# Sixteen transform tiles laid out by the groups of the last inverse stage, with a new order of the steps

## The chip, the core and the metric

The kernel runs on one core of a Trainium2 chip. The metric is the device time of one execution in microseconds. Five engines work side by side, each through its own list of instructions in order: TensorE (PE, matmuls; PEld is its weight load), VectorE (DVE), ScalarE (ACT), GpSimd (POOL) and SyncE (SP), which here only issues transfers. An engine waits for another, or for a transfer, by semaphores.

## The reference

```python
x = A_x                                          # [1, 2048, 512], float32
g = sigmoid((x * gate_w).sum(-1, keepdims=True))
a = irfft2(rfft2(x) * (w_r + 1j * w_i), s=(2048, 512))
h = gelu(einsum("bsd,df->bsf", x, w1) + b1)      # D 512, F 1792, tanh form
b = einsum("bsf,fd->bsd", h, w2) + b2
return g * a + (1 - g) * b
```

## The kernel before

Branch a is a two-dimensional Fourier transform, a product with W and the inverse; branch b is an MLP; the gate g mixes them.

The 2048 rows are taken as 16 tiles of 128. Matmuls transform along the 512 columns (`pd`, `ph`, `py`) and, at the end, along the 128 rows of a tile and back along the columns (`pz`, `pa`, `po`); between them a 16-point transform runs *across* the tiles, on DVE, as two stages of radix 4 forward and two inverse. The tile `y` holds all of it: 128 partitions, 16 tiles `Y[j]`, two components each, 257 columns. The groups of four tiles are

- `stage1(j0)`: tiles j0, j0+4, j0+8, j0+12, on DVE;
- `filt(q0)`: the second forward stage, the product with W (`m`, L771), `merge` (L780) and the first inverse stage, on tiles 4·q0 to 4·q0+3, on DVE;
- `stage4(j0)`: the last inverse stage, on tiles j0, j0+4, j0+8, j0+12, on DVE (temporaries `d0…` to `d3…`, by group).

In each radix-4 step (`radix4`) the last two writes are paired: one instruction writes a component of the group's second tile and one of its fourth (`mixed`), as one access with a stride between the two (`y<-d1d,d1d` is the first paired write of group 1, into tiles 5 and 13; `y<-d1s` the second).

After a group's `stage4` its four rows 64 are corrected: SP reads them from the four tiles into the small tile `ownx` (L813), ACT scales a copy `ownz` (L814), DVE combines the two (L816), and SP writes them back (L819). `ownx3` is the one of group 3, tiles 3, 7, 11 and 15. Then `inverse(c, h)` takes the tiles: ACT makes `sw` from `y` (L832), DVE `pq` (L836), TensorE `pz`.

The MLP's matmuls use a scheme of sums and differences (tiles `uxB`, `nuB`, `fiveB`, `g_…`, `v…`). The raw rows of w2 arrive in `vr…` (L999, issued by SP); ACT copies half of one into `v0…` (L1006), and DVE forms `vs…` from both (L1004). The results of branch b go to the accumulator `bacc` in memory.

All of this is first recorded as a graph of 2146 steps. Each step belongs to one engine. A written table, `ORDER` (L122), lists the steps in the order in which they are emitted, and `SLOTS` (L208) gives each buffer its place in its pool. `schedule()` asserts that the order respects the true dependencies, which it knows by parts of buffers (three for each tile of `y`). The costs that `a`, `v`, `m` and `dma` hand to a step belong to the planner that made the table; with a table written out they move nothing. On emission a layer below adds the semaphore waits, from the memory that the instructions touch.

Of the kernel before, what the change touches and what calls it, by code (L numbers as in the profile page):

```python
# [16 lines left out]
P = 128  # L17
# [32 lines left out]
def _split(v):  # L50
    h = _round12(v)
    return h.astype(np.float32), _round12(np.asarray(v, np.float64) - h).astype(np.float32)


def _tables():
# [47 lines left out]
    for n in range(NJ):  # L103
        for r in range(2):
            for c in range(2):
                y = np.zeros((2, 2))
                y[r, c] = 0.5
                u = (y[0, 0] - y[1, 1]) + 1j * (y[1, 0] + y[0, 1])
                v = ((y[1, 0] - y[0, 1]) + 1j * (y[0, 0] + y[1, 1])) * -1j * np.exp(1j * np.pi * n / NJ)
                for q in range(4):  # L110
                    o = np.array([u, v]) * np.exp(-0.5j * np.pi * (n // 4 * q % 4))
                    fx[r, n, c, :, n % 4 + 4 * q] = np.stack([o.real, o.imag], 1)
# [238 lines left out]
def tile_kernel(ctx: ExitStack, tc: tile.TileContext, xt, xc, w1, w2, b1, b2, x0g, wf, wrev, out, consts):  # L351
# [229 lines left out]
    def forward(j):  # L581
# [67 lines left out]
        if j // 4 == 3:  # L649
            for k in range(2):  # L650
                o = j % 4 * 2 + k
                add("sp", 0.58, 5.0, lambda k=k, o=o: sp.dma_start(own.ap()[o * 8:o * 8 + 8, :ND], yy.ap()[0:P:HP, j % 4::4, k]),
                    [Y[i] for i in range(j % 4, NJ, 4)], [(own, o)])

# [724 lines left out]
```

## Time and profile before

| | |
|---|---|
| runs | 362.92, 364.76, 365.01 us, median 364.76 |
| the profiled execution | 364.13 us |
| its span, and what lies outside it | 362.3 us, 1.83 us |
| mean granted TensorE clock | 0.988 |
| instructions in the span | 5797 |
| HBM | 52.02 MB read, 17.31 MB written |

The span runs from the first to the last instruction of the trace. An engine is busy while one of its instructions runs; issuing transfers does not count. The granted clock is the share of full speed that TensorE's throttle allowed. In the rows, `ownx<-y` means that `ownx` is written from `y`, with the numbers of buffers left out.

### The profile page before, as it was taken

The numbers are of one execution on the slowest core, as the hardware profiler recorded it, in microseconds if no ns is written. First come the engines' busy times: TensorE is split into PE (matmuls) and PEld (weight loads), VectorE is DVE, ScalarE is ACT, GpSimd is POOL, SyncE is SP. The second block draws the span as 40 slices with busy tenths as digits, with TensorE's granted clock in tenths as the row PEclk, the third lists the DMA queues.
The fourth block names the chain that finished last, engine by engine and source line by source line (L and its number), as shares of the span: only waits on it lengthen the run. The fifth ranks groups of instructions, "written<-read, shape, count | busy, mean of one in ns | idle before, by whom it ended". The sixth has DMA issues, their size and how long they took to land.

```text
span 362.3 us, 5797 instructions
## 1 busy us (share of the span) xinstructions
PE 348.5 (96%) x1742; PEld 293.5 (81%) x1742; DVE 337.0 (93%) x700; ACT 302.1 (83%) x631; POOL 56.5 (16%) x75
## 2 busy tenths in 40 slices
PE   6999999999999999999999999999869999999993
PEld 5988887888878888888888888888758888788782
DVE  4999998899999999999999999999678999999992
ACT  4999999999998677797888848799399999989732
POOL 1011002100013002000231400001010000443430
PEclk9999999999999999999999999999969999999998
DMA  7998969868697979998988865426756635599987
GB/s 216 358 296 207 359 193 267 180 215 231 176 302 148 281 213 224 254 318 218 249 211 219 145 152 189 154 88 233 148 102 178 177 130 161 88 155 213 170 184 238
DMA packets 47719, 74.63 MB, mean 206 GB/s; under 512 B 5544, under 2 KB 18344, under 8 KB 47688
## 3 DMA queue, kind: packets, MB, share of 16 engines
q1 hardware_dynamic: 37528, 58.42, 49.8%
q0 software_dynamic: 9728, 15.51, 26.9%
q10 hardware_dynamic: 432, 0.33, 0.3%
q8 instruction: 14, 0.23, 0.3%
q14 instruction: 17, 0.14, 0.1%
HBM read 52.02 MB, written 17.31 MB: 191 GB/s over the span
## 4 chain that ended last, share of the span: by engine, by line
PE 90%; ACT 3%; DMA 2%; DVE 1%; issue 1%; SPq 1%; DVEq 0%; ACTq 0%
PE po L416 36%; PE uxA L416 9%; PE uxB L416 9%; PE nuB L416 7%; PE nuA L416 7%; PE pd L416 4%; PE pz L416 4%; PE ph L416 3%; PE py L416 3%; PE pa L416 3%; PE dx L416 2%; DMA cf<-cf 1%; DMA bacc<-s 1%; PE dn L416 1%; PE dm L416 1%
## 5 line engine op out<-in xcount | busy, mean ns | idle before, releaser
L964 ACT ACTIVATE po<-s 128x512 f32<-128x512 f32 x40 | 23.7, 602 | 1.8 <-DVE g_6l L472 0.8
L425 ACT ACTIVATE s<-po 128x512 f32<-128x512 f32 x40 | 23.4, 596 | 0.9 <-PE po L416 0.9
L832 ACT ACTIVATE sw<-y,keep 64x512 f32<-64x512 f32 x32 | 22.7, 720 | 0.6
L771 DVE TENSOR_TENSOR m<-y,wf 128x514 f32<-128x514 f32 x32 | 21.3, 689 | 0.4
L416 PEld LDWEIGHTS pd<-cf,w 128*128 128x128 f32 x128 | 17.8, 190 | 3.8 <-DVE cf L543 2.0
L416 PE MATMUL pd<-cf,w 128*128 128x129 f32 x128 | 19.2, 276 | 1.7 <-DVE cf L543 1.7
L416 PE MATMUL py<-zb,tf 128*128 128x258 f32 x96 | 20.3, 297 | 0.0
L416 PEld LDWEIGHTS pz<-tg,pq 128*128 128x128 f32 x128 | 18.3, 195 | 1.6
L416 PE MATMUL pz<-tg,pq 128*128 128x128 f32 x128 | 19.0, 278 | 0.0
L416 PE MATMUL pa<-zb,ci 128*128 128x256 f32 x96 | 17.9, 297 | 0.9 <-ACT od L425 0.9
L416 PEld LDWEIGHTS pa<-zb,ci 128*128 128x128 f32 x96 | 14.9, 192 | 3.8 <-ACT od L425 1.5
L416 PE MATMUL nuB<-xB,wB0h 128*128 128x512 f32 x56 | 17.5, 393 | 0.0
L416 PEld LDWEIGHTS py<-zb,tf 128*128 128x128 f32 x96 | 15.9, 189 | 2.0
L974 ACT ACTIVATE s<-po,b2t 128x512 f32<-128x512 f32 x16 | 11.2, 699 | 6.8 <-PE po L416 6.6
L416 PE MATMUL uxB<-xBt,wB 128*128 128x512 f32 x42 | 12.0, 430 | 4.5 <-DVE nuB L1227 4.5
L589 DVE TENSOR_TENSOR eo<-xf 128x256 f32<-128x256 f32 x32 | 12.7, 418 | 3.5 <-DMA xf<-in_x0g 3.4
L416 PE MATMUL nuA<-xA,wA0h 128*128 128x512 f32 x48 | 14.9, 392 | 0.0
L628 DVE TENSOR_TENSOR zb<-pd,zb 128x256 fp32r<-128x256 f32 x32 | 13.3, 419 | 0.9 <-ACT logit L627 0.9
L410 POOL DMA_DIRECT2D wA0l<-in_w x6 | 5.1, 847 | 57.6 <-ACT wA0l L477 25.3
L416 PEld LDWEIGHTS uxB<-xBt,wB 128*128 128x128 f32 x42 | 8.5, 208 | 6.6 <-DVE nuB L1227 4.9
L648 ACT ACTIVATE y<-pys 64x257 f32<-64x257 f32 x32 | 12.9, 415 | 0.5
L836 DVE TENSOR_TENSOR pq<-y,sw 128x256 f32<-128x256 f32 x32 | 12.8, 417 | 0.4 <-ACT sw L832 0.2
(595 smaller groups left out, 1274.3 us busy)
## 6 DMA issues: line engine op xcount, KB each, us to landing
wf<-in_wf SPq DMA_DIRECT2D x16, 257.0 KB, 3.8
xf<-in_xt SPq DMA_DIRECT2D x14, 256.0 KB, 5.6
tf<-tf SPq DMA_DIRECT2D x16, 192.0 KB, 4.0
wrA<-in_w SPq DMA_DIRECT2D x12, 256.0 KB, 4.7
xbA<-in_xc SPq DMA_DIRECT2D x8, 256.0 KB
xbB<-in_xc SPq DMA_DIRECT2D x8, 256.0 KB, 4.5
bacc<-s SPq DMA_DIRECT2D x8, 256.0 KB
w<-bacc POOLq DMA_DIRECT2D x8, 256.0 KB, 5.0
```

The source lines that it names most:

```text
L410: return add("pool", 0.92, 3.3, lambda: nc.gpsimd.dma_start(dst(), src(), accum_op=ALU.add), reads, writes, 2.2 * kb / 350)
L416: pe.matmul(ps, w, x, start=start, stop=stop, **more)
L425: a(lambda: act.activation(o.ap(), i.ap(), AF.Copy, scale=scale), n, [i], [o])
L589: v(lambda s=s, op=op: vec.tensor_tensor(eo.ap()[:, s], x.ap()[:, 0:2], x.ap()[:, 2:4], op=op), 256, [x], [(eo, s)])
L628: v(lambda c=c: vec.tensor_tensor(segs(xl, c), both(c), segs(xh, c), op=ALU.subtract), 256, [ps[c], (xh, c)], [(xl, c)])
L648: a(lambda o=o, i=i: act.activation(Y[j].ap()[o:o + HP, 1], pys.ap()[i:i + HP, 1], AF.Copy), 257, [(pys, 1)], [(Y[j], 1 + k)], more=0.07)
L771: v(lambda mk=mk, k=k, y=y, w=w: vec.tensor_tensor(mk.ap(), y.ap(), w.ap()[:, k:k + 1, :ND].to_broadcast([P, 2, ND]), op=ALU.mult), 514, [ ...
L832: a(lambda sw=sw, y=y, o=o, i=i: act.activation(sw.ap()[o:o + HP], y.ap()[i:i + HP], AF.Copy, scale=keep.ap()[i:i + HP]), 512, [y, keep, * ...
L836: v(lambda sw=sw, pq_=pq_, y=y, k=k, op=op: vec.tensor_tensor(pq_.ap()[:, k], y.ap()[:, k], sw.ap()[:, 1 - k], op=op), 256, [y, TURNED[c], ...
L964: a(lambda ps=ps, n=n, o=o: act.activation(ps.ap(), o.ap()[:, n], AF.Copy), size, [o], [ps], more=0.04)
L974: a(lambda o=o, ps=ps, q=q: act.activation(o.ap(), ps.ap(), AF.Identity, bias=b2t.ap()[:, q:q + 1]), 600, [b2t, ps], [o])
```

## The change

The tiles of `y` change places: tile j lies at place j % 4 · 4 + j // 4, so that the four tiles of a `stage4` group are neighbours, and those of a `filt` group lie four places apart. The accesses that name several tiles follow (the own-row reads of L652, `merge`, the read and write of rows 64, `less_y`), and so do the columns of the table `fx`, which writes all tiles' rows 0 and 64 back. The planner's figure for the `sw` copies goes from 0.165 to 0.195, and `ORDER` and `SLOTS` are made anew. The graph of steps and their dependencies are the same. Line numbers behind the new function are four higher.

```diff
+def place(j):
+    return j % 4 * 4 + j // 4
...
-                    fx[r, n, c, :, n % 4 + 4 * q] = np.stack([o.real, o.imag], 1)
+                    fx[r, n, c, :, place(n % 4 + 4 * q)] = np.stack([o.real, o.imag], 1)
...
 ORDER = """
-8 12 16 108 6 15 0 2 3 4 5 27 19 18 28 7 21 22 30 23 29 24 1 31 59 9 60 56 55 13 14 25 10 57 17 58 86 489 36 37 40 38
...
+0 2 8 15 12 108 6 9 489 1 31 32 60 18 7 19 20 28 27 30 22 21 16 17 490 59 491 13 14 10 29 23 496 62 107 55 3 56 24 58
...
-    Y = [View(yy, 3 * j, 3, lambda t, j=j: t[:, j]) for j in range(NJ)]
+    Y = [View(yy, 3 * j, 3, lambda t, j=j: t[:, place(j)]) for j in range(NJ)]
...
-    YP = [View(yy, 3 * j, 3, lambda t, j=j: packed(t[:, j])) for j in range(NJ)]
+    YP = [View(yy, 3 * j, 3, lambda t, j=j: packed(t[:, place(j)])) for j in range(NJ)]
...
-                add("sp", 0.58, 5.0, lambda k=k, o=o: sp.dma_start(own.ap()[o * 8:o * 8 + 8, :ND], yy.ap()[0:P:HP, j % 4::4, k]),
+                add("sp", 0.58, 5.0, lambda k=k, o=o: sp.dma_start(own.ap()[o * 8:o * 8 + 8, :ND], yy.ap()[0:P:HP, j % 4 * 4:j % 4 * 4 + 4, k]),
...
         def merge():
-            e = yy.ap()[:, 4 * q0:4 * q0 + 4]
+            e = yy.ap()[:, q0::4]
...
         def rows():
-            return yy.ap()[HP:HP + 1, j0::4].rearrange("p j a b -> p j (a b)")[:, :, :D]
+            return yy.ap()[HP:HP + 1, 4 * j0:4 * j0 + 4].rearrange("p j a b -> p j (a b)")[:, :, :D]
...
-                    [y, keep, *([TURNED[c]] if i else [])], [(sw, k)], more=0.165)
+                    [y, keep, *([TURNED[c]] if i else [])], [(sw, k)], more=0.195)
...
-            vec.tensor_tensor(x, x, yy.ap()[:, c + 4 * (q // 2)::8, q % 2, :2 * P], op=ALU.subtract)
+            vec.tensor_tensor(x, x, yy.ap()[:, 4 * c + q // 2:4 * c + 4:2, q % 2, :2 * P], op=ALU.subtract)
```

What the new order moves is seen in the engines' lists. First SP, about two thirds of the way through the program, where group 3's rows 64 are read. A row has the line, the kind, what is written from what, the shape, and in brackets the semaphores that the instruction waits for (DMAHW and DMASW are those of transfers). Before:

```order
L413 DMA wBtl2_3193<-su2_758 128x512 [waits DMAHW6_49,DMAHW2_49]
L813 DMA ownx3_3195<-y_322 4x1x512 [waits DMAHW7_49,DVE_49]
L999 DMA vr11_3197<-in_w2 128x512 [waits DMAHW0_49,PE_49]
L999 DMA vr12_3199<-in_w2 128x512 [waits DMAHW1_49,DMASW0_49,Activation_49]
L980 DMA bacc1_3135<-s11_774 128x512
L819 DMA y_322<-ownx3_3195 1x4x512 [waits DMAHW7_49,DMAHW3_49,DVE_49]
L825 DMA tg31_3281<-ti 128x256 [waits DMAHW4_49,PE_49]
```

The same place of the changed kernel, around its read of `ownx3`:

```order
L417 DMA wBtl2_3128<-su2_734 128x512 [waits DMAHW5_49,PE_49]
L817 DMA ownx3_3130<-y_264 4x1x512 [waits DMAHW6_49,DVE_49]
L417 DMA wBth2_3132<-su2_734 128x512 [waits DMAHW7_49,DMASW3_49,PE_49]
L417 DMA ci_3004<-ci 128x512 [waits DMAHW0_49]
L817 DMA ownx1_3203<-y_264 4x1x512 [waits DMAHW1_49,DMAHW2_49,DVE_49,Activation_49]
L823 DMA y_264<-ownx3_3130 1x4x512 [waits DMAHW6_49,DVE_49]
```

The two loads of w2 no longer stand behind the read of `ownx3`. In the changed kernel they come later on SP, behind the write back of `ownx1` (vr13 and vr12, for the same step of w2; vr11 belongs to the step before it):

```order
L823 DMA y_264<-ownx1_3203 1x4x512 [waits DMAHW7_49,DMAHW1_49,DVE_49]
L984 DMA bacc0_3279<-s02_572 128x512 [waits DMAHW0_49]
L1003 DMA vr13_3350<-in_w2 128x512 [waits PE_49]
L417 DMA wBth5_3432<-su5_1742 128x512 [waits DMAHW2_49]
L829 DMA tg11_3434<-ti 128x256 [waits DMAHW3_49,PE_49]
L417 DMA wBth6_3447<-su6_1502 128x512 [waits DMAHW4_49]
L1003 DMA vr12_3449<-in_w2 128x512 [waits DMAHW5_49,DMASW5_49]
```

Then ACT, at the step that copies vr12, `v06`. Before:

```order
L892 ACTIVATE wb4h_3191<-wb4l_raw_2918 128x512 [waits DMAHW4_49,DMAHW0_49]
L425 ACTIVATE uxB21_3202<-uxB20_3122 128x512 [waits DVE_49,PE_49]
L1006 ACTIVATE v06_3204<-vr12_3199 128x256 [waits DMAHW2_49,DMAHW1_49]
L915 ACTIVATE uxB10_2976<-uxB10_2976,b1t_350 128x512
L814 ACTIVATE ownz3_3207<-ownx3_3195,al_527 4x512 [waits DMAHW7_49,DVE_49]
L425 ACTIVATE fiveB2_3222<-nuB21_3212 128x512 [waits PE_49]
```

And in the changed kernel:

```order
L852 ACTIVATE zb0_88<-pz7_3404 128x4x128 [waits PE_49]
L836 ACTIVATE sw5_3421<-y_264,keep_1506 64x512 [waits DMAHW7_49]
L429 ACTIVATE s20_2868<-po2_200_3355 128x512 [waits PE_49]
L429 ACTIVATE s21_2805<-po2_210_3176 128x512 [waits PE_49]
L1010 ACTIVATE v06_3505<-vr12_3449 128x256 [waits DMAHW5_49,DVE_49]
L836 ACTIVATE sw13_3507<-y_264,keep_1506 64x512 [waits PE_49]
```

`v06` now stands among the steps of the last `inverse` calls, with `ownz3` far ahead of it. Third, SP at the start of the program, before (`x2` is two rows that read alike):

```order
L547 DMA b2t_80<-in_b2 128x4
L518 DMA xf4_105<-in_xt 128x256 x2
L523 DMA cf_125<-cf 128x258 x2
L491 DMA xf8_129<-in_xt 128x512
L907 DMA war0_136<-in_w1 128x256 x2
L413 DMA tf0_159<-tf 128x384
```

and changed:

```order
L551 DMA b2t_92<-in_b2 128x4
L522 DMA xf4_95<-in_xt 128x256
L911 DMA war0_97<-in_w1 128x256
L522 DMA xf4_95<-in_xt 128x256
L911 DMA war0_97<-in_w1 128x256
L527 DMA cf_124<-cf 128x258 x2
L495 DMA xf8_127<-in_xt 128x512
```

The two halves of `war0`, the first rows of w1, now go ahead of the table `cf`.

200 rows, old and new, of tables (ORDER, SLOTS) are left out of this document.

## The prediction

> **What bounds the kernel now.** I read the busy sums first, then the 40 slices, then the chain of work that ended last.
>
> ```profile
> PE 348.5 (96%) x1742; PEld 293.5 (81%) x1742; DVE 337.0 (93%) x700; ACT 302.1 (83%) x631; POOL 56.5 (16%) x75
> PEclk9999999999999999999999999999969999999998
> PE 90%; ACT 3%; DMA 2%; DVE 1%; issue 1%; SPq 1%; DVEq 0%; ACTq 0%
> ```
>
> TensorE (PE) is busy for 348.5 of 362.3 us, and 90% of the chain is PE. Only one slice inside the program, the 30th, has a granted clock below nine tenths. So TensorE sets the end, and something that makes it neither shorter nor less idle is worth nothing. The view of stretches tells where its idle time lies. Its columns are start:end, length, then busy time (count) of PE, weight loads, DVE, ACT and POOL, granted clock, DMA share and GB/s.
>
> ```profile
> 0.00:7.36 7.36, 4.55 (x12) 3.47 (x12) 2.83 (x13) 2.52 (x5) 1.71 (x12) 1.00 0.68 183
> 100.00:257.20 157.20, 157.20 (x696) 129.47 (x695) 154.92 (x299) 129.17 (x246) 24.19 (x28) 1.00 0.79 209
> 257.20:271.00 13.80, 9.33 (x40) 7.57 (x39) 8.25 (x15) 8.00 (x15) 1.72 (x2) 0.77 0.54 130
> 304.00:320.00 16.00, 15.81 (x89) 13.24 (x88) 15.43 (x34) 15.47 (x27) 5.87 (x6) 1.00 0.60 107
> 320.00:358.00 38.00, 35.99 (x187) 30.23 (x185) 34.96 (x64) 25.15 (x47) 14.21 (x14) 1.00 0.93 204
> 358.00:362.30 4.30, 0.00 (x0) 0.00 (x0) 0.00 (x0) 0.00 (x0) 0.00 (x0) 0.74 0.45 112
> ```
>
> From 100 to 257 TensorE has no gap at all. The head (7.36 − 4.55 = 2.81 us), the last stretches (0.19 and 2.01) and the tail (4.30) lose something each, and the stretch from 257 to 271 loses 4.47 in one piece, with the clock down. The view of waits names who waited there (engine, tile, line, what it waited for: sum, times, longest).
>
> ```profile
> PE uxB L416 <- DVE nuB L1227: 4.5, 1, 4.5
> ACT v L1006 <- DMA bacc<-s: 5.9, 1, 5.9
> ```
>
> The second row must not be taken at its word: the ACT step at L1006 reads `vr`, a load of w2, and not `bacc`, which merely landed last on the same queue. The timeline (start, us, engine, line, operation) of SP, DVE, ACT and PE in this stretch tells the rest.
>
> ```profile
> 249.98 0.32 SPq L413 DMA_DIRECT2D wBtl<-su  x1
> 257.60 0.63 SPq L813 DMA_DIRECT2D ownx<-y  x1
> 258.35 0.83 SPq L999 DMA_DIRECT2D vr<-in_w  x2
> ...
> 244.47 1.29 DVE L680 SCALAR_TENSOR_TENSOR y<-d3s,d3s 128x512 f32<-128x512 f32 x2
> 256.89 0.68 DVE L680 SCALAR_TENSOR_TENSOR y<-d1d,d1d 128x512 f32<-128x512 f32 x1
> ...
> 256.47 0.58 ACT L425 ACTIVATE uxB<-uxB 128x512 f32<-128x512 f32 x1
> 262.95 0.42 ACT L1006 ACTIVATE v<-vr 128x256 fp32r<-128x256 f32 x1 [5.91 <-DMA bacc<-s]
> 263.85 0.70 ACT L814 ACTIVATE ownz<-ownx,al 4x512 f32<-4x512 f32 x1
> 264.46 0.57 ACT L425 ACTIVATE fiveB<-nuB 128x512 f32<-128x512 f32 x1
> ...
> 266.12 2.93 PE L416 MATMUL uxB<-xBt,wB 128*128 128x512 f32 x6 [4.47 <-DVE nuB L1227]
> ```
>
> SP issues nothing from 250.30 to 257.60. It stands at the read of group 3's rows 64 (L813). That group's own tiles (3, 7, 11, 15) had their last write at 244.47 + 1.29 = 245.76. SP goes 0.03 us after the end of another write, `y<-d1d` (256.89 + 0.68 = 257.57), which is of group 1 and touches tiles 5 and 13 alone: none of group 3's, but between them in memory. So the order is made by the range from a strided access's first to its last byte, and the wait is a **false** one. Behind it in SP's queue stand the loads vr11 and vr12. ACT, free at 256.47 + 0.58 = 257.05, has vr12's copy (v06) as its very next step and stands until 262.95. Behind that copy on ACT stand `ownz` and `fiveB`, on these DVE waits, and on DVE TensorE. From SP's read to TensorE's restart it is one chain.
>
> **The change part by part.** *Instructions.* None is added or removed. Each engine's count and shapes are the same in both orders (1597 matmuls, 630 ACT, 700 DVE, 257 SP and 62 POOL transfers), so PE's 348.5 us of work stay. The row 64 transfers remain 4x1x512.
>
> *The planner's figure 0.165 to 0.195.* The order is a written table, so this figure moves no instruction by itself. 0.
>
> *The layout.* In the new one group 3's tiles are neighbours, and no other group's write lies inside their range; the ordered read of ownx3 now follows the last write of its own group. The price of the false wait comes from these rows.
>
> ```profile
> 261.65:266.12 4.47, 0.00 (x1) 0.01 (x1) 1.54 (x4) 3.14 (x7) 0.22 (x1) 0.82 0.07 25
> 266.12:271.20 5.08, 5.08 (x15) 4.20 (x16) 4.40 (x8) 5.02 (x10) 1.51 (x2) 0.50 0.84 171
> 271.20:276.00 4.80, 4.80 (x31) 4.29 (x31) 4.76 (x9) 4.34 (x8) 0.00 (x0) 0.98 0.68 195
> ```
>
> First the idle time, 4.47. Then the clock, granted at 0.50 for 5.08 us after it: 5.08 × (1 − 0.50) = 2.54 more. Sum 7.01. As a check on whether the stall would go if only the false wait did: SP would be free at 250.30; the load's landing took from 258.75 (the second of its pair) to 262.95, 4.2 us; issued about 251.5, vr12 would land at 255.7, and ACT asks for it at 257.05. The stall would go whole, with 1.3 us to spare. What is late next? Behind 271 TensorE runs full (4.80 of 4.80), and nothing else waits there, so the time gained is not taken back at once.
>
> The Trainium skill, "TensorE: Matmul & The Clock Gate", Part 1: The HAM clock gate, says that the clock falls to half after at least one idle window of about 3.4 us and is whole again after about 3.4 us of work. By that the ramp would be worth about 1.7 instead of 2.54, and the forecast 0.8 higher; the row here shows 5.08 us at 0.50, and the measurement decides. By the same sentence a hold shorter than the window would leave the clock alone, which no row of this stretch can show.
>
> *The new order.* v06 no longer stands right behind a row 64 read: in the new order ACT has 21 instructions between the SP read's gate and v06. Two things come nearer instead. vr13 and vr12 now go behind the write back `y<-ownx1`, which waits for DVE, and DVE's use of both (`vs6`) stands 18 instructions behind that gate: ten of 512 columns and eight of 256. By rows
>
> ```profile
> 258.09 0.42 DVE L836 TENSOR_TENSOR pq<-y,sw 128x256 f32<-128x256 f32 x1
> 258.43 0.68 DVE L979 SCALAR_TENSOR_TENSOR s<-gb,s 128x512 f32<-128x512 f32 x1
> 259.03 0.69 DVE L678 TENSOR_TENSOR d0d<-y 128x512 f32<-128x512 f32 x1
> ```
>
> their starts lie 0.60 and 0.34 apart, 10 × 0.60 + 8 × 0.34 = 8.7 us. SP has six issues from that gate to vr12's: at 0.32 to 0.63 each (rows above) some 2.7 with the gate's own, and 4.2 to land is 6.9. Slack about 1.8, so 0; if it were lost, the price is in the rivals. At the head the halves of war0 come ahead of the two cf loads on SP:
>
> ```profile
> 2.15 0.91 SPq L523 DMA_DIRECT2D cf<-cf  x2
> 3.58 0.91 SPq L907 DMA_DIRECT2D war<-in_w  x2
> ```
>
> Two issues of 0.46 put cf's second half about 0.95 us later, while TensorE has eight early matmuls (about 0.9 us) it can do before. I take 0; the bounds are 0 (it cannot gain, since nothing is loaded sooner that TensorE waits for) and +1.1 (cf's delay whole, with 0.2 for landings beside one another). For the rest of the new order no row prices anything. It can win at most the gaps of 304 to 358, 0.19 + 2.01 = 2.2, since the other stretches have none; it can lose by leaving TensorE some other gap in which the clock falls, and I bound this by the 2.54 of the row above. I take 0, nearest to the stretches without gaps, which are most of the program.
>
> *The strided side.* One group must be strided: now it is the filter stage's (tiles q0, q0+4, …, where they were neighbours), the merge at L780 and less_y at L989. Their shapes are the same, and the readers and writers of `y` in the filter stage are all on DVE, which runs in order anyway, so a false order there holds nobody. 0; a rival prices it.
>
> *Sum.* 364.13 (the profiled execution; 362.3 of span and 1.83 outside it) − 4.47 − 2.54 = **357.1**. The runs' median is 364.76, 0.63 higher, inside their spread of 2.09, so no correction is made. About 1% (3.6 us, hence 361.1) is what a measurement of this kernel can tell from no change.
>
> **The rivals.** *A new hold takes the old one's place.* v06 or vs6 waits again, since vr13 and vr12 stand behind a DVE-gated write back. For it: DVE is 98.5% busy up to 257 (154.92 of 157.20), so a late DVE step makes SP late at once. Against it: 1.8 us of slack, and that DVE is the waiter and the gate both. A hold as long as the old idle piece without the drop of the clock gives 357.1 + 4.5 = 361.6; a shorter one lies between.
>
> *The change doesn't do what it says.* The read is held for another reason than the range, or the stall only moves along the chain to the next late thing. For it: the 0.03 us between `y<-d1d` and the read might be chance, and order and layout differ at once. Against it: a second such pair,
>
> ```profile
> 240.62 0.87 DVE L816 SCALAR_TENSOR_TENSOR ownx<-ownx,al,ownz 4x256 f32<-4x256 f32 x2
> 242.86 0.68 DVE L680 SCALAR_TENSOR_TENSOR y<-d3d,d3d 128x512 f32<-128x512 f32 x1
> 243.57 0.66 SPq L819 DMA_DIRECT2D y<-ownx  x1
> ```
>
> group 2's write back, whose data were ready at 241.49, goes 0.03 us after group 3's write ends at 243.54. Time: 364.1, give or take the 1.8 between the fastest run and the median.
>
> *Slower: the false ranges move to the filter stage.* Its eight paired writes (two for each of four groups) now span the other groups' tiles, while TensorE and DVE have no slack (157.20 and 154.92 of 157.20). If ACT copies or transfers of `y` were still under way there, each would be held as ownx3 was, at 4.47. Two such holds give 357.1 + 8.9 = 366.0, no change; it decides from three on: 357.1 + 13.4 = 370.5. Against it: the order shows only DVE at `y` in that stage.
>
> **How the numbers follow.** The forecast, the hold gone with nothing in its place, has 0.68, with a range of its own of 354.9 (less 2.2) to 359.6 (plus 2.54). A new hold 0.15, no effect 0.11, slower 0.06. The range has to reach past the forecast's own into the new hold; with about 1 us, half the spread of the runs, on both sides: 354.9 − 1.0 to 361.6 + 1.0, **353.9 to 362.6**. It leaves out nearly all of "no effect" and "slower" and some edges, about 0.2. Faster by over 1%: 0.68 and half of the new hold, 0.76. Within 1%: the other half and nearly all of no effect, 0.17. Slower: 0.07.
>
> **What would show it.** In the changed profile the row of L1010's wait for a DMA is gone, no stretch behind 240 has TensorE idle for over 1 us, no slice but the head's and tail's has a clock below nine tenths, and the read of ownx3 starts within some 0.1 us of the end of group 3's own last write or of SP's issue before it. PE's busy time falls by about 2.5, to 346. The forecast is wrong if ACT or DVE still waits for `vr` by more than 1 us, if the idle piece stays and only its releaser has another name, or if waits for ACT show in the filter stage.

## The result, and the profile after

| | runs | median us | ratio to before, 95% interval |
|---|---|---|---|
| before, beside the changed kernel | 4 | 364.36 (362.92 to 365.01) | |
| changed | 4 | 358.35 (357.80 to 358.85) | 0.984, 0.981 to 0.987 |

The forecast was 357.1 with a range of 353.9 to 362.6. The profiled execution of the changed kernel has a span of 356.6 us, 5.7 below the 362.3 of before.

The page of the changed kernel, its rows for the busy sums, the granted clock by slices and the chain that ended last:

```profile
PE 348.4 (98%) x1742; PEld 291.6 (82%) x1742; DVE 336.6 (94%) x700; ACT 303.5 (85%) x631; POOL 56.8 (16%) x75
PEclk9999999999999999999999999999999999999998
PE 62%; ACT 17%; DVE 15%; issue 4%; DVEq 0%; ACTq 0%
```

The slice with the lower clock is gone. The chain now runs through ACT and DVE for a third of its length: TensorE is busy for 98% of the span, and the last releaser of a step is now often ACT or DVE. The view of stretches (length, busy of PE, weight loads, DVE, ACT, POOL, granted clock, DMA share, GB/s) shows where TensorE's idle time went:

```profile
0.00:7.36 7.36, 6.29 (x24) 4.97 (x25) 3.51 (x14) 3.26 (x6) 1.76 (x12) 1.00 0.71 191
240.00:257.20 17.20, 17.03 (x77) 13.55 (x76) 17.06 (x34) 16.22 (x29) 2.64 (x3) 1.00 0.73 197
257.20:271.00 13.80, 13.75 (x80) 11.30 (x79) 13.32 (x27) 13.51 (x24) 0.85 (x1) 1.00 0.33 88
271.00:304.00 33.00, 32.57 (x196) 28.34 (x195) 31.26 (x72) 32.30 (x57) 0.94 (x2) 1.00 0.63 185
```

From 257 to 271, 4.47 of idle became 0.05, and the clock is 1.00. The head lost 2.81 and now loses 1.07. Small gaps are new: 0.17 before 257 and 0.43 from 271 to 304, where there were none. The timeline of SP, DVE and ACT around the read of `ownx3`, whose line is now L817:

```profile
247.57 0.32 SPq L417 DMA_DIRECT2D wBtl<-su  x1
247.99 0.63 SPq L817 DMA_DIRECT2D ownx<-y  x1
...
246.35 0.67 DVE L684 SCALAR_TENSOR_TENSOR y<-d3s,d3s 128x512 f32<-128x512 f32 x1
...
282.35 0.42 ACT L1010 ACTIVATE v<-vr 128x256 fp32r<-128x256 f32 x1
279.38 0.42 DVE L1008 TENSOR_TENSOR vs<-vr,vr 128x256 f32<-128x256 f32 x1
```

The read goes 0.10 us behind the end of SP's issue before it (247.57 + 0.32 = 247.89), and its own group's last write had ended at 247.02. `v06` (the ACT row) and `vs6` (the last) run without a wait: no bracket at the row's end.

### The profile page after: what moved, and what is told of

Read it like the earlier page. It is cut to its first block, busy times and chain, and to the rows that moved or that the text cites. A ratio compares the mean times of both kernels' runs of the same rounds, so it can differ in the third digit from the quotient of the medians.

```text
span 356.6 us, 5786 instructions
## 1 busy us (share of the span) xinstructions
PE 348.4 (98%) x1742; PEld 291.6 (82%) x1742; DVE 336.6 (94%) x700; ACT 303.5 (85%) x631; POOL 56.8 (16%) x75
## 4 chain that ended last, share of the span: by engine, by line
PE 62%; ACT 17%; DVE 15%; issue 4%; DVEq 0%; ACTq 0%
PE po L420 21%; PE uxB L420 7%; PE uxA L420 6%; PE nuB L420 5%; PE nuA L420 5%; PE ph L420 4%; PE pd L420 3%; PE dx L420 3%; PE py L420 3%; ACT sw L836 2%; PE pa L420 2%; DVE y L682 1%; DVE y L680 1%; PE none L420 1%; PE pz L420 1%
## 5 line engine op out<-in xcount | busy, mean ns | idle before, releaser
L420 PEld LDWEIGHTS pz<-tg,pq 128*128 128x128 f32 x128 | 17.5, 190 | 1.7 <-DVE pq L840 0.3
L420 PE MATMUL pa<-zb,ci 128*128 128x256 f32 x96 | 17.1, 292 | 1.5 <-DVE zb L853 1.0
L652 ACT ACTIVATE y<-pys 64x257 f32<-64x257 f32 x32 | 13.2, 416 | 0.6
L596 DVE TENSOR_TENSOR w<-eo 128x256 f32<-128x256 f32 x32 | 12.8, 419 | 0.3
L414 POOL DMA_DIRECT2D w<-bacc x8 | 10.9, 1369 | 9.3 <-DVE w L881 3.4
```

The source lines that it names most:

```text
L414: return add("pool", 0.92, 3.3, lambda: nc.gpsimd.dma_start(dst(), src(), accum_op=ALU.add), reads, writes, 2.2 * kb / 350)
L420: pe.matmul(ps, w, x, start=start, stop=stop, **more)
L596: v(lambda s=s, op=op: vec.tensor_tensor(w.ap()[:, s], eo.ap()[:, :, 0], eo.ap()[:, :, 1], op=op), 256, [eo], [(w, s)])
L652: a(lambda o=o, i=i: act.activation(Y[j].ap()[o:o + HP, 1], pys.ap()[i:i + HP, 1], AF.Copy), 257, [(pys, 1)], [(Y[j], 1 + k)], more=0.07)
```

## The experiments

The times first. "Stretch" is read from each run's TensorE timeline: from the start of the last `uxB<-xB,wBtl` ahead of the hold to the start of the second `po<-g_2h,wb2h` behind it, the same matmuls each time. It comes from one execution of each kernel, the profiled one. For the kernels in the new order these matmuls do not follow each other, so there is none. Ratios are to the kernel before, on the same chip.

| run | median us (runs) | ratio, 95% interval | stretch us |
|---|---|---|---|
| before, beside each batch | 363.68, 363.73, 363.80 (17, 22, 20) | | 11.29 |
| new layout, old order | 357.95 (6) | 0.9839, 0.9805 to 0.9873 | 4.13 |
| old layout, new order | 359.03 (4) | 0.9869, 0.9834 to 0.9903 | |
| read listed early | 357.65 (6) | 0.9842, 0.9803 to 0.9881 | 4.14 |
| read listed between the two paired writes | 362.26 (12) | 0.9969, 0.9943 to 0.9995 | 9.42 |
| loads first | 362.04 (12) | 0.9946, 0.9926 to 0.9966 | 7.89 |
| store first | 362.00 (12) | 0.9956, 0.9938 to 0.9975 | 9.04 |
| loads and store first | 359.01 (6) | 0.9879, 0.9853 to 0.9905 | 5.66 |
| idle piece filled | 362.57 (12) | 0.9983, 0.9964 to 1.0002 | 10.23 |
| new layout, new head | 357.38 (6) | 0.9831, 0.9807 to 0.9856 | 4.13 |
| whole change, again | 358.52 (6) | 0.9854, 0.9830 to 0.9878 | |
| whole change, head put back | 361.32 (9) | 0.9932, 0.9907 to 0.9958 | |

The stretch falls by more than the medians do: by 7.16 against 5.7 with the new layout alone, and by 3.40 against 1.6 with the loads first, whose profiled execution (363.42) was the slowest of its twelve.

The stretch rows of before, and then of the new layout with the old order:

```profile
261.26 0.39 PE L416 MATMUL uxB<-xB,wBtl 128*128 128x512 f32 x1
272.55 0.39 PE L416 MATMUL po<-g_2h,wb2h 128*128 128x512 f32 x1
```

```profile
260.94 0.39 PE L420 MATMUL uxB<-xB,wBtl 128*128 128x512 f32 x1
261.17 1.52 PE L420 MATMUL uxB<-xBt,wB 128*128 128x512 f32 x6
265.07 0.39 PE L420 MATMUL po<-g_2h,wb2h 128*128 128x512 f32 x1
```

### The two halves of the change

**The layout alone**: the diff of the change without `ORDER`, `SLOTS` and the planner's figure.

> The new layout of y with the order and slots of before. Theory A (the read of ownx3 is held by the range over group 1's paired writes, and that hold is worth 4.47 idle + 2.54 of halved clock): the read goes near 250.3, right behind SP's issue before it, v06 no longer waits on ACT, the idle piece at 262 to 266 and the slice of lower clock are gone; 357.4 us (364.4 - 7.0). Theory B (the hold has another cause, and only the new order removes it): 364.4, with the idle piece at the same place. Theory C (the strided filter groups cost something): over 358 with the idle piece gone, and the loss between 100 and 240.

Theory A held: 357.95, a stretch 7.16 shorter, and no idle piece. SP and ACT in this run:

```profile
247.86 0.32 SPq L417 DMA_DIRECT2D wBtl<-su  x1
248.27 0.62 SPq L817 DMA_DIRECT2D ownx<-y  x1
249.02 1.58 SPq L1003 DMA_DIRECT2D vr<-in_w  x2
250.95 0.33 SPq L984 DMA_DIRECT2D bacc<-s  x1
...
256.65 0.41 ACT L1010 ACTIVATE v<-vr 128x256 fp32r<-128x256 f32 x1
```

The read goes right behind SP's last issue, everything behind it follows at once, and `v06` finds its inputs there. The price of the strided side (theory C) shows nowhere: from 100 to 257.2 TensorE is as full as before,

```profile
100.00:257.20 157.20, 157.20 (x696) 129.41 (x695) 154.87 (x299) 129.13 (x247) 24.20 (x28) 1.00 0.80 213
```

**The order alone**: `ORDER` and `SLOTS` of the change in the old layout.

> The new order and slots with the old layout. Theory A: the range of ownx3's read still takes in tiles of other groups, but in the new order no other group's paired write stands between its own last write and the read, and v06 is 21 ACT steps away, so nothing is held: 358.4 as for the whole change, 359 at most. Rival (the layout is what brings the gain, whatever the order): 364 to 365, with a hold of SP at a read of ownx.

SP's read in the timeline, and TensorE's stretch:

```profile
248.36 0.63 SPq L813 DMA_DIRECT2D ownx<-y  x1
...
257.20:271.00 13.80, 13.76 (x79) 11.34 (x78) 13.37 (x27) 13.51 (x25) 0.85 (x1) 1.00 0.39 101
```

There is no hold at the read either, which goes 0.10 us behind SP's issue before it (248.36): 359.03. So each half removes the hold by itself, and the two do not add up. The whole change (358.35, and 358.52 when run again) is no faster than the layout alone.

### What made the read late, and what waited behind it

**The read listed early**: one step is listed ahead of group 1's first paired write.

```diff
-1412 1887 1015 1819 … 1855 1419 1884 1849 1337 1994 2009 1047
+1337 1412 1887 1015 1819 … 1855 1419 1884 1849 1994 2009 1047
```

(1337 is the read of `ownx3`, 1412 and 1413 group 1's paired writes, 1994 and 2009 the loads vr11 and vr12, 1047 the store of s11 to `bacc`, 1849 the load SP issues ahead of the read.)

> Before, with one step moved: the read of ownx3 is listed ahead of group 1's first paired write, so that the old layout's range finds no foreign write. Theory A: the read goes behind its own group's last write (245.8), vr11 and vr12 by 252, no idle piece; 357.4. Rival (the read is late for its queue or for the chip, not for the foreign write): 364.4. If only TensorE's idle time counts and the halved clock costs nothing: 359.9.

It measured 357.65, with the old layout and the old order but for this step, and the read goes at 245.40, 0.02 us behind its own group's last write (244.09 + 1.29 = 245.38).

**The read listed between the two paired writes** leaves every engine's own list as it is:

```diff
-1857 1413 1410 1299 1006 1855 1419 1884 1849 1337 1994 2009 1047
+1857 1849 1337 1413 1410 1299 1006 1855 1419 1884 1994 2009 1047
```

> Before, with every engine's list of instructions as it was; the read of ownx3 and the SP load ahead of it are only listed before group 1's second paired write (256.9) instead of behind it, so that the range finds the first one (252.76 + 0.68) as the last foreign write. Theory A: the read goes within 0.1 us of that write's end, some 4.1 sooner than before; v06 starts near 258.8 and still waits 1.7; TensorE idles 0.4 or less with the clock at 1.0, and has some 1.2 of ACT's backlog behind it, as with all_first: 359.0. Rival (the read's time is not set by the paired writes): the read stays near 257.6, 363.7.

SP, DVE, ACT, POOL and PE in the timeline of this run:

```profile
253.00 0.62 SPq L813 DMA_DIRECT2D ownx<-y  x1
253.75 0.91 SPq L999 DMA_DIRECT2D vr<-in_w  x2
254.70 0.43 SPq L980 DMA_DIRECT2D bacc<-s  x1
...
252.29 0.69 DVE L680 SCALAR_TENSOR_TENSOR y<-d1d,d1d 128x512 f32<-128x512 f32 x1
...
261.44 0.42 ACT L1006 ACTIVATE v<-vr 128x256 fp32r<-128x256 f32 x1 [4.86 <-DMA bacc<-s]
...
252.12 0.88 POOL L410 DMA_DIRECT2D wb3l<-in_w  x1 [41.01 <-ACT wb3l L477]
252.67 1.21 POOL L410 DMA_DIRECT2D wb2l<-in_w  x1
...
264.61 2.80 PE L416 MATMUL uxB<-xBt,wB 128*128 128x512 f32 x6 [3.43 <-DVE nuB L1227]
```

The first step of the theory held to 0.02 us: the read goes at 253.00, and the *first* paired write ends at 252.29 + 0.69 = 252.98. Nothing but the listing had changed, so the read's time is set by whichever write inside its range is listed last ahead of it. Not every write of `y` counts. Both paired writes of group 1 show as `y<-d1d,d1d`; a row `y<-d1s,d1s`, which the description of the kernel before calls the second of them, is a write of a single tile. In the kernel before one of these, step 1410, is listed ahead of the read too:

```profile
257.49 0.68 DVE L680 SCALAR_TENSOR_TENSOR y<-d1s,d1s 128x512 f32<-128x512 f32 x1
```

It writes tile 1, which lies ahead of tile 3 and so outside the read's range (tiles 3 to 15), and the read goes at 257.60 without waiting for its end at 258.17.

The second step failed. The loads and the store left SP 4.5 us sooner (0.5 of it because this execution ran ahead of the one of before by that much all along), but `v06` started only 1.5 sooner, at 261.44; its row names the store, which left last. POOL's two accumulating loads had been issued just ahead of them, and the landing time in the view of transfers for this stretch is

```profile
vr<-in_w SPq DMA_DIRECT2D x2, 256.0 KB, 6.5
```

against 3.2 for the same pair in the same view of before, where POOL's loads had gone some 4 us earlier (the last by 254.35, the pair at 258.35):

```profile
vr<-in_w SPq DMA_DIRECT2D x2, 256.0 KB, 3.2
```

That the transfers shared the DMA engines with POOL's is how I read this; no run took POOL's loads away. With the layout alone the pair leaves by 250.60 (249.02 + 1.58), ahead of POOL's first load (252.28 there), and nothing is late.

**Loads first, store first, and both** (old layout; the read stays behind both paired writes):

```diff
-1849 1337 1994 2009 1047
+1849 1994 2009 1337 1047      (loads first)
+1849 1047 1337 1994 2009      (store first)
+1849 1047 1994 2009 1337      (loads and store first)
```

> Before, with the loads vr11 and vr12 listed ahead of the read of ownx3 on SP; the false wait of the read stays. Theory A (what costs is what stands behind the read, first of all v06 on ACT): v06 starts near 257.1; ownz3 becomes the next to wait, for a read that still goes at 257.6 and lands 2.4 to 4.2 later; TensorE starts again 2.3 after that, at 262.3 to 264.1, an idle piece of 0.6 to 2.4 without the halved clock: 358.0 to 359.8. Rival (the read itself is what all wait for): 364.4.

Loads first was a miss in its mechanism, and the most useful run. SP, ACT and PE:

```profile
252.35 0.91 SPq L999 DMA_DIRECT2D vr<-in_w  x2
258.95 0.62 SPq L813 DMA_DIRECT2D ownx<-y  x1
259.93 0.33 SPq L980 DMA_DIRECT2D bacc<-s  x1
...
262.35 0.42 ACT L1006 ACTIVATE v<-vr 128x256 fp32r<-128x256 f32 x1 [3.95 <-DMA bacc<-s]
...
265.52 1.67 PE L416 MATMUL uxB<-xBt,wB 128*128 128x512 f32 x6 [2.47 <-DVE nuB L1227]
```

vr12 left SP by 253.26, yet `v06` still started at 262.35, 2.4 behind the issue of the store of s11. `v06` is written into the place in memory that s11 held, so it waits for that store as well as for its load, and the row of before said so: `bacc<-s`. TensorE's idle piece was 2.47, and from its restart to the second `po<-g_2h` this run takes 5.03 us (265.52 to 270.55).

> Before, with one step moved: the store of s11 to bacc listed ahead of the read of ownx3. The run with the loads first showed that v06 also waits for this store (v06 takes s11's place in memory). Theory D (v06 waits for both the load of vr12 and that store, and both stand behind the read): with the store alone ahead, vr12, still issued near 259 behind the read, lands 2.4 to 4.2 later and holds v06 until 261.4 to 263.2: 362 to 364. Rival (the store alone was the wait, and vr12's landing is early): v06 at 260 or sooner, under 361.

SP, ACT and PE with the store first:

```profile
250.48 0.42 SPq L980 DMA_DIRECT2D bacc<-s  x1
257.21 0.62 SPq L813 DMA_DIRECT2D ownx<-y  x1
257.96 0.84 SPq L999 DMA_DIRECT2D vr<-in_w  x2
...
261.33 0.42 ACT L1006 ACTIVATE v<-vr 128x256 fp32r<-128x256 f32 x1 [4.67 <-DMA vr<-in_w]
...
264.49 2.93 PE L416 MATMUL uxB<-xBt,wB 128*128 128x512 f32 x6 [3.21 <-DVE nuB L1227]
```

Now the load is the last to come: 362.00. Each alone gains 1.6 to 1.7 us, by medians.

> Before, with the store of s11 and the loads vr11 and vr12 all listed ahead of the read of ownx3; only the false wait of the read itself stays, with ownz3 for its one waiter. Theory D: v06 starts at 257.1; the read goes at 257.6, lands 2.4 to 4.2 later, ownz3 at 260.1 to 262.1, TensorE again 2.3 behind it: an idle piece of 0.6 to 2.7 and no halved clock: 358 to 360.5. Rival (nothing is left once v06 is free): 357.5 to 358. Rival (the read's lateness alone makes the stall): 363.7.

ACT and PE with both first:

```profile
256.45 0.41 ACT L1006 ACTIVATE v<-vr 128x256 fp32r<-128x256 f32 x1
259.07 0.72 ACT L814 ACTIVATE ownz<-ownx,al 4x512 f32<-4x512 f32 x1 [1.66 <-DMA ownx<-y]
...
261.36 1.66 PE L416 MATMUL uxB<-xBt,wB 128*128 128x512 f32 x6 [0.22 <-DVE nuB L1227]
```

With both ahead, 359.01. `v06` is free, and the read itself, still held, makes ACT wait for 1.66 and TensorE for 0.22; with ACT's backlog behind that the stretch is 1.5 longer than with the read listed early (5.66 against 4.14), and the time 1.4 longer by medians. So the false wait on a transfer of 8 KB cost about a quarter by itself; what stood behind it in SP's queue cost the rest, 4.7 of 6.0.

### The halved clock

**The idle piece filled**: in the kernel before, `uxB` step 1862 is listed seven steps sooner, and a `pz` step is repeated behind it, writing the same values again.

```diff
             s.emit()
+            if s.n == 1862:
+                for _ in range(10):
+                    g.steps[1272].emit()
```

> Before, with the hold left as it is, and 20 matmuls of pz2 repeated by TensorE in the idle piece (they write the same values again; one uxB step is listed seven steps sooner so that they stand behind it). They take about 2.2 us and leave some 2.2 idle. If the idle length makes the clock fall: it stays at 1.0 behind the gap, and the time is 2.5 lower, 361.2. If the clock falls by any wait of that chain, or the halved stretch costs nothing by itself: 363.7.

The repeats came to 40 matmuls in the trace, not 20, and filled nearly all of the piece, which does no harm to the question. PE's timeline:

```profile
260.71 4.62 PE L416 MATMUL pz<-tg,pq 128*128 128x128 f32 x40
265.69 1.66 PE L416 MATMUL uxB<-xBt,wB 128*128 128x512 f32 x6 [0.35 <-DVE nuB L1227]
268.03 0.50 PE L416 MATMUL pa<-zb,ci 128*128 128x256 f32 x2 [0.68 <-ACT zb L848]
270.72 0.39 PE L416 MATMUL po<-g_2h,wb2h 128*128 128x512 f32 x1
```

The six matmuls take 1.66 instead of 2.93, so the clock stayed whole, and the hold itself stayed (265.69 against 266.12). But the stretch is only 1.06 shorter (10.23), and the time 1.2 lower by medians, with an interval that touches no change. The reason is mostly the third row: at the whole clock TensorE now meets a wait of 0.68 for ACT, which had been hidden under the slower matmuls.

The runs of before point the same way without any edit. Of the 59 beside the batches, 18 have a mean clock of 0.993 or more and 34 one of 0.989 or less. The difference in clock, 0.007 of some 362 us, is 2.5 us of full speed, yet their mean times, 363.2 and 364.2, lie only 1.0 apart. In which stretch their clocks differed is not on record.

### The head

**The new layout with the old order and the new head**:

```diff
-… 56 55 13 14 25 10 57 17 58 86 489 36 37 …
+… 56 55 489 490 13 14 25 10 57 17 58 86 496 497 498 36 37 …
```

(489 and 490 are war0's loads, 13 and 14 cf's, 496 to 498 `ph` steps, 36 the first `pd` step.)

> The new layout with the order of before, and of the new order only the head: war0's halves ahead of cf on SP, and the first three ph steps (12 matmuls) ahead of pd on TensorE. If the head is worth what the slices of the changed kernel show (TensorE loses 2.8 there instead of 3.6 to 4.0): 0.8 to 1.2 below the layout alone, 356.8 to 357.2, which beats both kernels. If the forecast's term was right (0 to +1.1): 358.0 to 359.1.

357.38 against 357.95, between what the two theories gave and with ranges that overlap, so a gain is not shown. In the profiled executions `pd` starts 0.78 later than with the layout alone (7.70 against 6.92), as `cf` comes later, but `ph` matmuls fill the wait: up to 20 us TensorE is busy for 18.48 instead of 17.51.

**The whole change, as it is and with its head put back** (the loads of cf ahead of war0's, and steps 496 to 498 behind `pd`):

> The changed kernel as it is, beside the next one on one chip. From the runs so far: 358.0 to 358.7, so that it lies level with the layout alone (357.95) and the order alone (359.03); if the gains of layout and order added up it would have to be near 353.

> The changed kernel with its head put back: cf ahead of war0's halves on SP, and the first three ph steps behind the first pd steps on TensorE. If the new head gives 1.2 (TensorE's loss in the first slice is 2.8 against 4.0 before): 359.5. If what it gains at the start is lost by 20 us, as layout_head had it, or if the term of the forecast (0) was right: level with the whole change within 0.5.

The changed kernel repeats at 358.52. With its head put back, it is 2.8 slower (361.32), more than double what either theory gave. Its first `pd` matmuls and the stretches of its first 20 us, and then the stretches of the whole change:

```profile
7.54 0.49 PE L420 MATMUL pd<-cf,w 128*128 128x129 f32 x2 [2.11 <-DVE cf L547]
...
0.00:7.54 7.54, 4.36 (x11) 3.18 (x11) 3.80 (x16) 2.93 (x6) 1.75 (x12) 1.00 0.70 189
7.54:20.00 12.46, 12.46 (x88) 12.18 (x89) 9.82 (x28) 8.80 (x33) 0.00 (x0) 0.86 0.83 289
```

```profile
0.00:7.54 7.54, 6.47 (x26) 5.61 (x27) 3.99 (x17) 3.25 (x6) 1.76 (x12) 1.00 0.70 186
7.54:20.00 12.46, 12.46 (x88) 11.21 (x87) 12.02 (x35) 10.91 (x39) 0.89 (x1) 1.00 1.02 374
```

Without the early `ph` matmuls TensorE idles 2.11 longer at the start (6.47 − 4.36), and the clock behind that averages 0.86, worth another 1.7 (12.46 × 0.14). The two come to 3.8, while the spans lie 2.9 apart (359.9 and 357.0), so not all of it reaches the end. Nor does the clock explain every run: of the nine, two kept a mean clock of 0.999 or more, and they measured 358.88 and 361.32. This head is not quite that of before, whose `ph` steps stood one by one between others, so the run bears on what the fill is worth in the new order, and does not tell what the new head gained over the old.

## Why the prediction was right, and where it was not

**The false wait by range: right.** Moving the foreign write out of the range (layout alone), or the read ahead of the write (read listed early), gives the same 4.13 and 4.14; moving the read from the second paired write to the first moves its issue to 0.02 us behind the first; and a write outside the range does not hold it.

**The sum of 7.01: right in total.** The stretch fell by 7.16, and the spans of the two profiled executions by 7.1 (355.2 for the layout alone). Its TensorE is busy for 346.3, as forecast. The medians fell by 5.7, with an interval of 0.9805 to 0.9873, so 4.6 to 7.1. The spans flatter the sum: the profiled execution of before (364.13) lies 0.45 above the median of before beside this run, that of the layout alone (356.95) 1.0 below.

**The term "2.54 for the clock": mis-attributed.** From TensorE's restart to the second `po<-g_2h` a clean pass takes 3.90 us (261.17 to 265.07). Before, it took 6.43, 2.53 more. With the clock whole but the hold left it took 5.03 (265.69 to 270.72), 1.13 more, and the same 5.03 in loads first, where the clock stayed whole by itself. So the clock alone was worth 1.4 of it; the rest was ACT's backlog from the same hold, which lay under the slow matmuls. Taking the hold away removes both, which is why the sum still came out.

**"The second row must not be taken at its word": wrong.** It named the store to `bacc`, and I took that for an accident of the queue. Loads first showed that the store was a wait of its own, as late as the load. So the landing time of 4.2 for vr12, taken up to the start of `v06`, was mis-read as well: the store ended that wait, and the view of transfers gives 3.2 for the loads. The forecast did not suffer, because both stood behind the same read.

**"Nothing takes its place": right for the hold.** vr12 and vr13 behind `y<-ownx1` did not hold anyone. "No stretch behind 240 has TensorE idle for over 1 us" just about held: the longest wait there is this one,

```profile
PE pa L420 <- DVE zb L853: 1.0, 1, 1.0
```

**The head, "0, it cannot gain": wrong by its reason.** `war0` is loaded sooner, and the new head fills TensorE's idle start with `ph` matmuls: 1.07 of idle in place of 2.81 in the profiled executions. That term should have had a bound below nothing; the row that shows the idle start stood in the prediction. What of it reaches the end is open (357.38 against 357.95, ranges overlapping).

**The rest of the new order, "0": slightly too good.** The whole change lies 0.4 to 0.6 above the layout alone, by medians from two chips, which these runs do not tell from nothing. Its TensorE is busy for 348.4 instead of the 346 that I forecast, and it has the new small gaps; which of its moves cost these I did not take apart. The forecast was low by 1.25 (358.35 against 357.1): 0.40 of it is this, and 0.85 is the layout alone (357.95), whose runs gained 5.7 where the sum had 7.0 from a start 0.45 higher.

**The other rivals.** "No effect" is out by the layout alone. "Slower, by false ranges in the filter stage" is out by the full 157.20 from 100 to 257.2. The new layout with the new head (357.38) is the lowest time of all, about 1 us below the whole change; they ran on different chips.

## What to carry to other kernels

When a queue stands still, look for what ended in the last few hundredths of a microsecond before it goes on, and compare the addresses: where dependencies are taken by the range of a strided access, an unrelated write inside the range orders it, and either a layout or one step listed elsewhere frees it. Count what stands behind the held instruction in its queue, since that set the price here, and take the name in a row of waits for real until an experiment says otherwise. When a hold and its aftermath are priced, the terms may overlap (a slow engine hides another's backlog), so the sum holds for removing the cause and not for treating one term.

## What the runs showed of the hardware

The clock fell to half behind an idle piece of 3.21 us (store first) and of 3.43 (the read between the writes), but not behind one of 2.47 (loads first). The rows of TensorE's restart stand with these runs: its six matmuls take 2.93, 2.80 and 1.67 us. The Trainium skill, "TensorE: Matmul & The Clock Gate", Part 1: The HAM clock gate, gives about 3.4 us as the window and calls it free-running; an idle piece of 3.21 that is enough, and one of 2.47 that is not, are close to that, though 3.21 lies under it. The head does not fit so well. Put back, it idles for 2.11 us ahead of `pd`, and the clock behind that still fell. In the profiled execution of loads first, whose head is that of before,

```profile
7.11 1.84 PE L416 MATMUL pd<-cf,w 128*128 128x129 f32 x10 [1.80 <-DVE cf L543]
```

the clock is at 0.50 from 8 to 11 us behind an idle piece of 1.80, while before kept it whole behind 1.75. So the length of one idle piece does not decide it there, and what does is open; each of these rows is one execution.

A pair of loads of 256 KB each landed 3.2 us after issue in one run (median of the two) and 6.5 in another, with POOL's accumulating loads issued just ahead of it; the cause was not isolated.
